# A float32 attention and two gated layers on one core: the v_in product as seven block products per pair of row blocks, the v_out product in four parts of K

## The chip, the cores and the metric

The kernel runs on one core of a Trainium2 chip. The metric is the device time of one execution in microseconds (us); several runs are timed and their median is compared. Engines: TensorE (PE; its weight loads are the row PEld), VectorE (DVE), ScalarE (ACT), GpSimd (POOL) and SyncE (SP), whose queue issues all the DMAs of this kernel.

## What is computed

Causal attention over 2 batches, 12 heads, 448 positions and head size 64 gives x (896 tokens by 768). Two layers follow; in the kernel w_out of the first is already folded into its w3, and the names v_in and v_out stand for `moe2_w_in` and `moe2_w_out`.

```python
def _moe_ref(x, w1, w2, w3, w_out):
    a = x @ w1
    b = x @ w2
    h = a * b @ w3
    return (h @ w_out).astype(np.float32)

def _moe2_ref(x, w_in, w_out):          # w_in 768 x 2048, w_out 2048 x 768
    h = x @ w_in
    relu6 = np.clip(h + 3.0, 0.0, 6.0)
    g = h * relu6 / 6.0
    return (g @ w_out).astype(np.float32)
```

The products keep float32 accuracy on TensorE by splitting every operand into a high and a low part in the float32r type, so that each 128x128 block product is three matmuls (high times high, high times low, low times high). The weights arrive as 64-bit floats; ScalarE and VectorE put the bits together.

## The kernel before, in words

All activations are held transposed: features on the 128 partitions, tokens along the free axis, in two batches b of S = 448 columns. One matmul therefore moves 448 columns through a 128x128 weight block.

The program records every operation in a `Plan` with an engine, an estimated cost, its reads and writes and a rank. `Plan.issue` then plays a list schedule with these costs and writes the instructions out in the order that it finds; each engine runs its own queue strictly in that order. Work of the last layers has rank `DENSE + n`, with n the index of a weight unit in the list `units`. `ahead(n)` fetches unit n + 3 and converts unit n + 2 after unit n.

The stages, in order:

- Attention, with the product of w3 and w_out (`weights_product`, tile pw) beside it and after it.
- The product with w1 and w2, tiles paX, paY and paZ (`first`, `second`, `multiply`). Here both are already computed as a 2x2 block product with seven block products: a pair consists of one block column of w1 and one of w2, the inner dimension of 768 falls into two halves of HK = 3 blocks, and the two batches are the other side. `combine` forms the block sums of the weights (S1 to S4, A11, A12, A22) and `moving` those of the activations (tiles T1 to T4). P1 to P7 in `side` name which is multiplied by which; one of them is 3 blocks times 3 matmuls.
- The product px with the folded weights (tile wp, line 770), three groups of two row blocks and two batches in four PSUM banks; `keep` (lines 645 to 651) splits each result into the high and low parts of x2t, by a ScalarE copy (line 647) and a VectorE subtraction (line 649).
- The product with v_in, tile pg (line 635): 16 row blocks m, 2 batches, KD = 6 blocks, 3 matmuls, each result going through `hswish` (ScalarE, VectorE, ScalarE, VectorE, lines 656 to 662) into gt[m], of which all 16 are kept.
- The product with v_out, tile po (line 811): 6 row blocks, two halves of KF = 8 blocks, 2 batches, 3 matmuls; the 16 blocks of K accumulate in one PSUM bank, and `store` copies it out (lines 669 and 671) and sends it by DMA (line 673).

Converting one unit of v_in takes two operations on VectorE and one on ScalarE for the bits (`bits`: lines 279, 286, 289) and one on each for the split (`split`: lines 259 and 261). The tiles "raw" (RAWS = 3) hold what a DMA brought, the tiles "hl" (HLS = 4) what is ready for TensorE; in `combine` the second of a pair has a tile "raw2" with two buffers. PSUM has 8 banks, 2 in the pool `pd` (tag "d") and 6 in the pool of tag "dl". The pair of tiles "a1" and that of "a2" are scratch for results on their way.

Of the kernel before, what the change touches and what calls it, by code (L numbers as in the profile page):

```python
# [34 lines left out]
DENSE = 100.0  # L35
# [6 lines left out]
EARLY, LATE = 0, 1.0  # L42
# [112 lines left out]
def attention_moe_moe2(ctx: ExitStack, tc, q, k, v, w1, w2, w3, w_out, v_in, v_out, out):  # L155
# [19 lines left out]
    HK = KD // 2  # L175
    SCALE = 1.0 / float(D) ** 0.5
# [55 lines left out]
    def fetch(plan, n, rank):  # L232
# [4 lines left out]
        if name == "w2":  # L237
            raw = plan.tile(lambda: later["t"].tile([P, KD * P, 2], U32, tag="raw2", name=f"{name}r{m}", bufs=2),
                            "raw2", 2, (done,))
            raw2s.append(raw)  # L240
        else:
            raw = plan.tile(lambda: ws.tile([P, KF * P, 2], U32, tag="raw", name=f"{name}r{m}", bufs=RAWS), "raw", RAWS)
# [50 lines left out]
    def convert(plan, n, rank):  # L293
# [3 lines left out]
        if name == "w1":  # L297
            return
        raw, size = raws.pop(n)
        if name == "w2":  # L300
            combine(plan, m, raws.pop(n - 1)[0], raw, rank)
# [15 lines left out]
    def combine(plan, f, r1, r2, rank):  # L317


        size, h = KD * P, KD * P // 2  # L320
        bits(plan, r1, size, rank, True)
        low = lambda r, i, k=1: f32(r[:, i * h:(i + k) * h, 0])
        high = lambda r, i, k=1: f32(r[:, i * h:(i + k) * h, 1])
        first, second, third, fourth = (parts(f"{c}", f) for c in ("wa", "wb", "wc", "wd"))
        split(plan, first, 0, size, lambda: low(r1, 0, 2), [r1.at("l")], rank)
        bits(plan, r2, size, rank, True)

        def add(eng, dst, reads, write, a, b, op):
# [300 lines left out]
    def product(ps, n, kt, x, keys):  # L629
        hl = hls[n]  # L630
        mm = list(passes(kt))
        for kk in range(kt):
            def go(kk=kk):
                for _, a, c, st, sp in mm[3 * kk:3 * kk + 3]:
                    nc.tensor.matmul(ps[:, :S], weight(n, a, kk), x(kk, c), start=st, stop=sp)  # L635

            plan.op("pe", 0.6, go, reads=[hl, *keys(kk)], writes=[ps], rank=DENSE + n)

# [6 lines left out]
    def keep(ps, t, b, n):  # L645

        plan.op("act", act(S), lambda: nc.scalar.copy(part(t, HI, b), ps[:, :S]),
                reads=[ps], writes=[t.at((b, HI))], rank=DENSE + n)
        plan.op("dve", dve(S), lambda: nc.vector.tensor_tensor(
            part(t, LO, b), ps[:, :S], f32(part(t, HI, b)), ALU.subtract),  # L650
            reads=[ps, t.at((b, HI))], writes=[t.at((b, LO))], rank=DENSE + n)

    def hswish(ps, t, m, b, n):
        r = scratch("a1", f"r_{m}_{b}")
        g6 = scratch("a2", f"g6_{m}_{b}")
        plan.op("act", act(S), lambda: nc.scalar.activation(r[:, :], ps[:, :S], AF.Relu, bias=three, scale=1.0),  # L656
# [224 lines left out]
```

## Time and profile before

| | us |
|---|---|
| median of 3 runs | 572.93 |
| the three runs | 573.76, 572.93, 569.14 |
| the profiled execution's own time | 571.27 |
| its span, from the first to the last instruction | 569.3 |

The profile comes from one execution. The time of that execution is 1.97 us longer than its span. In the profile's views a matmul's start is measured and its end is modelled, so two matmuls that follow each other overlap in their rows; the distance of their starts is what one costs. TensorE's granted clock is given as a share of 2.4 GHz.

### The profile page before, as it was taken

The page shows a single profiled execution, that of the slowest core. Times are in us where ns is not written, and L with a number is a line of the kernel's source. Part 1 is how long each engine was busy: PE and PEld are TensorE (multiplying, and loading weights), DVE is VectorE, ACT ScalarE, POOL GpSimd, SP SyncE. Part 2 cuts the span into 40 slices and gives each one's busy share as a digit, 9 for nine tenths or more (in the row PEclk, how much of TensorE's full clock was granted, in tenths as well). Part 3 has the DMA queues.
Part 4 walks back from the last instruction along what each step waited for, and adds up shares of the span by engine and source line. Part 5 has one row for each costly group of instructions (what it writes and reads, how often), then busy time and mean ns, then how long its engine had stood idle before and what let it go on. Part 6 is the DMA issues. An engine that isn't in the chain of part 4 may idle for free.

```text
span 569.3 us, 7756 instructions
## 1 busy us (share of the span) xinstructions
PE 555.1 (98%) x2900; PEld 494.1 (87%) x2900; DVE 326.1 (57%) x583; ACT 283.2 (50%) x556; POOL 111.8 (20%) x142
## 2 busy tenths in 40 slices
PE   6899999999999999999999999999999999999997
PEld 4576757878999998999999999999999999999996
DVE  3677776855952978887633547666667643331000
ACT  4587877776815557764331335555556522220100
POOL 4556546642140323331000000000000000000000
PEclk8799999999999999999999999999999999999999
DMA  8666685724514233321603324333243433430000
GB/s 318 225 196 220 224 276 200 237 71 129 170 50 139 93 125 115 112 94 37 202 1 112 111 76 145 108 114 109 101 153 124 143 149 119 152 107 16 17 32 33
DMA packets 22853, 73.38 MB, mean 129 GB/s; under 512 B 2080, under 2 KB 11296, under 8 KB 20256
## 3 DMA queue, kind: packets, MB, share of 16 engines
q1 hardware_dynamic: 22816, 72.88, 37.8%
q8 instruction: 23, 0.38, 0.3%
q14 instruction: 14, 0.11, 0.1%
HBM read 66.98 MB, written 5.90 MB: 128 GB/s over the span
## 4 chain that ended last, share of the span: by engine, by line
PE 70%; DVE 3%; DMA 2%; ACT 1%; issue 0%; ACTq 0%; DVEq 0%; SPq 0%
PE po L811 20%; PE pg L635 20%; PE px L770 10%; PE pw L553 7%; PE paX L696 7%; PE paZ L696 3%; PE paY L696 2%; DMA w1r<-in_moe_w 1%; DVE wd L261 1%; DMA w2r<-in_moe_w 1%; DVE w1r L289 1%; DVE ab L724 0%; DVE w1r L330 0%; PE o L490 0%; PE ptp L465 0%; ACT w1r L279 0%
## 5 line engine op out<-in xcount | busy, mean ns | idle before, releaser
L635 PE MATMUL pg<-x2t,vi 128*128 128x448 f32 x576 | 115.4, 362 | 0.0
L811 PE MATMUL po<-g,vo 128*128 128x448 f32 x576 | 115.4, 362 | 0.0
L635 PEld LDWEIGHTS pg<-x2t,vi 128*128 128x128 f32 x576 | 108.0, 188 | 7.2
L811 PEld LDWEIGHTS po<-g,vo 128*128 128x128 f32 x576 | 108.0, 188 | 7.2
L553 PE MATMUL pw<-wr,w 128*128 128x384 f32 x384 | 75.8, 347 | 0.0
L443 POOL TENSOR_SCALAR prb<-prb,sums 128x448 f32<-128x448 f32 (+6 forms) x84 | 59.7, 727 | 54.9 <-DVE sums L437 52.2
L553 PEld LDWEIGHTS pw<-wr,w 128*128 128x128 f32 x384 | 66.0, 188 | 1.7
L770 PE MATMUL px<-ab,wp 128*128 128x448 f32 x288 | 57.9, 362 | 0.0
L416 PE MATMUL s<-ks,qs 128*128 128x448 f32 (+6 forms) x168 | 53.2, 428 | 4.1 <-DMA ks<-in_k 3.3
L770 PEld LDWEIGHTS px<-ab,wp 128*128 128x128 f32 x288 | 54.0, 188 | 3.6
L423 ACT ACTIVATE prb<-z,sums 128x448 f32<-128x448 f32 (+6 forms) x84 | 42.1, 506 | 5.7 <-DVE sums L419 5.5
L416 PEld LDWEIGHTS s<-ks,qs 128*128 128x128 f32 x168 | 29.4, 203 | 14.9 <-DVE sums L419 5.1
L419 DVE CUSTOM_DVE_ANT_0 z<-s,maskb 128x448 f32<-128x448 f32 (+6 forms) x84 | 33.2, 418 | 15.1 <-PE s L416 8.6
L656 ACT ACTIVATE r<-pg,consts 128x448 f32<-128x448 f32 x32 | 20.3, 635 | 33.2 <-PE pg L635 33.2
L279 ACT ACTIVATE vor<-vor 128x1024 f32<-128x1024 f32 x12 | 14.0, 1164 | 36.9 <-DMA vor<-in_moe_w_out 36.9
L473 ACT COPY pt<-ptp 128x512 f32<-128x512 f32 (+1 forms) x48 | 24.7, 561 | 14.9 <-PE ptp L465 14.7
L658 DVE SCALAR_TENSOR_TENSOR g<-r,pg 128x448 f32<-128x448 f32 x32 | 19.8, 619 | 19.7 <-ACT r L656 19.6
L465 PEld LDWEIGHTS ptp<-ident,prb 128*128 128x128 f32 x192 | 22.0, 141 | 10.0 <-POOL prb L443 5.0
L465 PE MATMUL ptp<-ident,prb 128*128 128x128 f32 x192 | 25.9, 276 | 4.3 <-POOL prb L443 4.2
L490 PE MATMUL o<-pt,vr 128*64 128x448 f32 (+3 forms) x192 | 26.9, 396 | 0.0
L669 ACT COPY out<-po 128x448 f32<-128x448 f32 x6 | 3.2, 534 | 47.1 <-PE po L811 29.3
L671 DVE COPY out<-po 128x448 f32<-128x448 f32 x6 | 3.8, 627 | 39.8 <-PE po L811 39.8
(103 smaller groups left out, 786.7 us busy)
## 6 DMA issues: line engine op xcount, KB each, us to landing
vir<-in_moe_w_in SPq DMA_DIRECT2D x16, 768.0 KB, 4.3
vor<-in_moe_w_out SPq DMA_DIRECT2D x12, 1024.0 KB, 4.9
w3r<-in_moe_w SPq DMA_DIRECT2D x8, 1024.0 KB, 6.7
wrr<-in_moe_w_out SPq DMA_DIRECT2D x8, 768.0 KB, 5.9
w1r<-in_moe_w SPq DMA_DIRECT2D x8, 768.0 KB, 5.8
w2r<-in_moe_w SPq DMA_DIRECT2D x8, 768.0 KB, 4.3
qs<-in_q SPq DMA_DIRECT2D x12, 448.0 KB, 3.4
vr<-in_v SPq DMA_DIRECT2D x12, 256.0 KB, 3.4
```

The lines of the kernel that those rows point to most:

```text
L416: plan.op("pe", pe4(n), lambda: nc.tensor.matmul(ps[:, :n], qs[u][:, t].rearrange("p h i -> p (h i)"), ks[u][:, :n], start=True, stop=True ...
L419: plan.op("dve", dve(n) + 0.09, lambda: nc.vector.tensor_tensor_reduce(out=z[:, :n], in0=ps[:, :n], in1=maskb[:, S - n:], scale=-SCALE, sc ...
L423: plan.op("act", act(n, True) + 0.2, lambda: nc.scalar.activation(pb[:, OFF[t]:OFF[t] + n], z[:, :n], AF.Exp, bias=sm[:, 0, t:t + 1], scal ...
L443: nc.gpsimd.tensor_scalar(s, s, sm[:, 1, t:t + 1], 1.0, ALU.mult, ALU.mult)
L465: nc.tensor.transpose(ps[:w, i * P:(i + 1) * P], pb[:, OFF[t] + kb * P:OFF[t] + kb * P + w], ident)
L473: plan.op("act", act(cut), lambda: nc.scalar.copy(dst()[:, :cut], ps[:, :cut]), reads=[ps], writes=[d.at((g, 0))], rank=rank)
L490: nc.tensor.matmul(ps[T * j:T * j + T, kb * P:S], vr[u][:w, kb, j, :], d[:w, base[kb]:base[kb] + TQ - 2 * kb, j, :], start=kb == 0, stop=k ...
L553: nc.tensor.matmul(ps[:, :W], weight(n, a, kk), hls[1 + kk][:, c, h * W:(h + 1) * W], start=kk == 0 and a == c, stop=kk == KF - 1 and a == LO)
L635: nc.tensor.matmul(ps[:, :S], weight(n, a, kk), x(kk, c), start=st, stop=sp)
L696: nc.tensor.matmul(ps[:, :S], hl[:, a, off + kk * P:off + (kk + 1) * P], t[:, c], start=first and kk == 0 and a == c, stop=kk == HK - 1 an ...
L770: nc.tensor.matmul(ps[m, b][:, :S], weight(n, a, kk), ab[kk][:, c, cols(b)], start=kk == 0 and a == c, stop=kk == KF - 1 and a == LO)
L811: nc.tensor.matmul(ps[:, :S], weight(n, a, kk), gt[k][:, c, cols(b)], start=k == 0 and a == c, stop=k == KF2 - 1 and a == LO)
```

## The change

The product with v_in takes the form that the product with w1 and w2 already has. Row blocks 2f and 2f + 1 of v_in make a pair (units "vi" and "vj"), eight pairs in all, and `gated(f)` computes both row blocks for both batches by P1 to P7 in three PSUM banks X, Y and Z, with sums on the way taken by ScalarE copies (`keep_sum`) and VectorE additions (`add_sum`). The 2x2 blocks of x2 come from px: its groups are now rows p and p + 3 together, and `differences` forms T1 to T4 from the four PSUM banks of a group and a scratch tile x2s, beside the three blocks of x2t that are needed as they are.

`combine` serves both products. For v_in ("vj") its four additions all run on VectorE, its two wide high-part copies on GpSimd (before, the additions of w1 and w2 are half on GpSimd and the copies on ScalarE), and three of the seven weight blocks (S2, A22, S4) go into tiles of one buffer each (`own`).

The product with v_out is cut into four parts c of KC = 4 blocks of K. Part c needs only the pairs 2c and 2c + 1, so gt shares the buffers of ab, 8 blocks instead of 16. The list `work` sets the order: pairs 0 and 1; then for each part the next pair, a third of part c - 1, the next pair, and the two other thirds; at the end the three thirds of the last part. A third is two row blocks m and one unit of v_out in a new layout (512 rows by 256 columns). Since a bank no longer holds the whole sum, `evict` copies the result of part 0 to a tile o (ScalarE) and writes it to DRAM (`sums_of`); for parts 1 to 3 o is fetched from DRAM first, VectorE adds the bank to it, and it goes back to DRAM or, in the last part, to the output.

`hswish` works in place on one scratch tile and reads its input from SBUF for three of the four results of a pair. The SBUF set aside for descriptors of dynamic DMAs is halved (1024 instead of 2048). The functions `product` and `store`, the old loops over m and `turn3` are gone. The diff, cut to its core:

```diff
+    KC = 4
+    NC = KF2 // KC
...
-    units += [(None, KF, m, "wp") for m in range(KD)]
-    units += [(v_in, KD, m, "vi") for m in range(KF2)]
-    units += [(v_out, KF, n, "vo") for n in range(2 * KD)]
-    raws, hls, comb, raw2s = {}, {}, {}, []
+    units += [(None, KF, m, "wp") for p in range(HK) for m in (p, p + HK)]
+    work = [("pg", 0), ("pg", 1)]
+    for c in range(1, NC):
+        work += [("pg", 2 * c), ("po", c - 1, 0), ("pg", 2 * c + 1), ("po", c - 1, 1), ("po", c - 1, 2)]
+    work += [("po", NC - 1, i) for i in range(HK)]
+    for w in work:
+        first_of[w] = len(units)
+        if w[0] == "pg":
+            units += [(v_in, KD, 2 * w[1], "vi"), (v_in, KD, 2 * w[1] + 1, "vj")]
+        else:
+            units.append((v_out, KF, w[2] * NC + w[1], "vo"))
...
-        if name == "w2":
+        if name in ("w2", "vj"):
...
+        beside = f[0] == "vj"
+        adds, eng = (("dve",) * 4, "pool") if beside else (ADDS, "dve")
...
+        def own(i):
+            return plan.tile(lambda: xp.tile([P, 2, S], F32R, tag=f"x{i}_1", name=f"v{i}_{f[1]}"), f"x{i}_1", 1)
+        first, second = (parts(f"{f[0]}{c}", f[1]) for c in "ab")
+        if beside:
+            s2, a22, s4 = ((own(i), 0) for i in range(3))
+        else:
+            s2, a22 = ((parts(f"{f[0]}{c}", f[1]), 0) for c in "cd")
+            s4 = a22[0], h
+        split(plan, first, 0, size, lambda: low(r1, 0, 2), [r1.at("l")], rank, eng)
...
+        split(plan, *s2, h, lambda: high(r1, 0), [H1], rank)
+        split(plan, second, 0, size, lambda: high(r2, 0, 2), [H2], rank, eng)
+        split(plan, *a22, h, lambda: low(r2, 1), [L2], rank)
+        split(plan, *s4, h, lambda: high(r1, 1), [H1], rank)
...
+    def evict(ps, m, b, n, c, o):
+        rank = DENSE + n
+        if c:
+            plan.op("dve", dve(S), lambda: nc.vector.tensor_tensor(o[:, :], ps[:, :S], o[:, :], ALU.add),
+                    reads=[ps], writes=[o], rank=rank)
+        else:
+            plan.op("act", act(S), lambda: nc.scalar.copy(o[:, :], ps[:, :S]), reads=[ps], writes=[o], rank=rank)
+        if c == NC - 1:
+            plan.op("sp", 0.6, lambda: nc.sync.dma_start(out[m * P:(m + 1) * P, cols(b)], o[:, :]),
+                    reads=[o], rank=rank)
+        else:
+            plan.op("sp", 0.6, lambda: nc.sync.dma_start(sums_of[m, b], o[:, :]),
+                    reads=[o], writes=[summed.at((m, b))], rank=rank)
...
+    def multiply(f, name, ps, first, rank, kind="w2"):
         a, *x = side[name]
-        hl, off = comb[f][a]
+        hl, off = comb[kind, f if kind == "w2" else 2 * f + 1][a]
+        xs = xt if kind == "w2" else x2
...
+    def differences(p, ps, rank):
+        s = plan.tile(lambda: xp.tile([P, 2, S], F32, tag=f"x{p}_1", name=f"x2s{p}"), f"x{p}_1", 1)
+        low, high = s.at(0), s.at(1)
+        plan.op("act", act(S), lambda: nc.scalar.copy(s[:, 0], ps[p, 1][:, :S]), reads=[ps[p, 1]], writes=[low], rank=rank)
+        for m, b in ((p, 0), (p + HK, 0), (p + HK, 1)):
+            x2[m, b] = plan.tile(
+                lambda m=m, b=b: xp.tile([P, 2, S], F32R, tag=f"x{m}_{b}", name=f"x2t{m}_{b}"), f"x{m}_{b}", 1)
+            keep(ps[m, b], x2[m, b], rank)
+        def less(i, bank, j):
+            plan.op("dve", dve(S), lambda: nc.vector.tensor_tensor(s[:, i], bank[:, :S], s[:, j], ALU.subtract),
+                    reads=[bank, s.at(j)], writes=[s.at(i)], rank=rank)
+        def whole(name, i):
+            t = plan.tile(lambda: later["t"].tile([P, 2, S], F32R, tag=f"{name}_{p}", name=f"{name}g_{p}"),
+                          f"{name}_{p}", 1, (done,))
+            plan.op("act", act(S, True), lambda: nc.scalar.copy(t[:, HI], s[:, i]),
+                    reads=[s.at(i)], writes=[t.at(0)], rank=rank)
+            plan.op("dve", dve(S), lambda: nc.vector.tensor_tensor(t[:, LO], s[:, i], f32(t[:, HI]), ALU.subtract),
+                    reads=[s.at(i), t.at(0)], writes=[t.at(1)], rank=rank)
+            tt[name, p] = t
+        less(1, ps[p + HK, 1], 0)
+        plan.op("dve", dve(S), lambda: nc.vector.tensor_tensor(s[:, 0], s[:, 0], ps[p, 0][:, :S], ALU.subtract),
+                reads=[ps[p, 0]], writes=[low], rank=rank)
+        whole("T1", 0)
+        less(0, ps[p + HK, 1], 0)
+        whole("T3", 1)
+        whole("T2", 0)
+        less(1, ps[p + HK, 0], 0)
+        whole("T4", 1)
...
+    sums_of = dp.tile([KD, B, P, S], F32, name="sums_of")
+    summed = Handle(plan, None, None, 0)
+    summed.ap = sums_of
...
+    def gated(f):
+        rank = DENSE + first_of["pg", f]
+        for m in (2 * f, 2 * f + 1):
+            tag = f"ab{m % KF}"
+            gt[m] = plan.tile(lambda m=m, tag=tag: later["ab"].tile([P, 2, NT], F32R, tag=tag, name=f"g{m}"),
+                              tag, 1, (done2,))
+        X, Y, Z = (dense_bank(f"pg{c}{f}") for c in "XYZ")
+        p1, c22, u2 = scratch("a1", f"q1_{f}"), scratch("a1", f"q22_{f}"), scratch("a2", f"q2_{f}")
+        def keep_sum(bank, x):
+            plan.op("act", act(S), lambda: nc.scalar.copy(x[:, :], bank[:, :S]), reads=[bank], writes=[x], rank=rank)
+        def add_sum(bank, x):
+            plan.op("dve", dve(S), lambda: nc.vector.tensor_tensor(x[:, :], x[:, :], bank[:, :S], ALU.add),
+                    reads=[bank], writes=[x], rank=rank)
+        multiply(f, "P1", X, True, rank, "vj")
+        keep_sum(X, p1)
+        multiply(f, "P2", Y, True, rank, "vj")
+        add_sum(Y, p1)
+        hswish(lambda: p1[:, :], p1, gt[2 * f], 0, rank + LATE)
+        multiply(f, "P6", X, False, rank, "vj")
+        keep_sum(X, u2)
+        multiply(f, "P5", Z, True, rank, "vj")
+        keep_sum(Z, c22)
+        multiply(f, "P7", X, False, rank, "vj")
+        add_sum(X, c22)
+        hswish(lambda: c22[:, :], c22, gt[2 * f + 1], 1, rank + LATE)
+        multiply(f, "P3", Z, False, rank, "vj")
+        add_sum(Z, u2)
+        hswish(lambda: u2[:, :], u2, gt[2 * f], 1, rank + LATE)
+        multiply(f, "P4", X, False, rank, "vj")
+        hswish(lambda: X[:, :S], X, gt[2 * f + 1], 0, rank)
+    def collected(c, i):
+        n = first_of["po", c, i]
+        for j in range(2):
+            m = 2 * i + j
             for b in range(B):
+                name = f"po{c}_{m}_{b}"
+                ps = dense_bank(name) if j else plan.tile(
+                    lambda name=name: pd.tile([P, 512], F32, tag="d", name=name), "psd", DENSE_BANKS)
+                o = scratch("a2", f"o{c}_{m}_{b}") if b else spare(f"o{c}_{m}_{b}")
+                if c:
+                    plan.op("sp", 0.6, lambda o=o, m=m, b=b: nc.sync.dma_start(o[:, :], sums_of[m, b]),
+                            reads=[summed.at((m, b))], writes=[o], rank=DENSE + n - 2)
+                for kk in range(KC):
+                    def go(ps=ps, n=n, at_=(kk * 2 + j) * P, k=c * KC + kk, kk=kk, b=b):
+                        for a, d in ((HI, HI), (HI, LO), (LO, HI)):
                             nc.tensor.matmul(
+                                ps[:, :S], hls[n][:, a, at_:at_ + P], gt[k][:, d, cols(b)],
+                                start=kk == 0 and a == d, stop=kk == KC - 1 and a == LO)
+                    plan.op("pe", 0.6, go, reads=[hls[n], *halves(gt[c * KC + kk], b)], writes=[ps], rank=DENSE + n)
+                evict(ps, m, b, n, c, o)
+    for w in work:
+        if w[0] == "pg":
+            gated(w[1])
+            for i in range(2):
+                ahead(first_of[w] + i)
+        else:
+            collected(*w[1:])
+            ahead(first_of[w])
     plan.issue()
+    right.close()
+    left.close()
...
+    if name == "moe2_w_out":
+        return _units(a, 512, 256)
```

The order of the instructions, as the planner writes it out. TensorE, where px ends and the product with v_in begins (px_0 and px_1 are banks of px by batch, wp and vi weights, x2t the activations; each row is three matmuls), before:

```order
L770 MATMUL px_1_3027<-ab_2780,wp_2889 128x448 x3
L770 MATMUL px_1_3033<-ab_2780,wp_2907 128x448 x3
L635 MATMUL pg_0_3141<-x2t_0_2871,vi_3017 128x448 x3
L635 MATMUL pg_0_3141<-x2t_0_2876,vi_3017 128x448 x3
L635 MATMUL pg_0_3141<-x2t_0_2999,vi_3017 128x448 x3
L635 MATMUL pg_0_3141<-x2t_0_3004,vi_3017 128x448 x3
L635 MATMUL pg_0_3141<-x2t_0_3127,vi_3017 128x448 x3
L635 MATMUL pg_0_3141<-x2t_0_3132,vi_3017 128x448 x3
```

And now, from the third row of the stage on (vja holds the blocks A11 and A12 of a pair, vjb S1 and S3, v_1 the block S2 of the first pair, T1g and T2g the block sums of x2):

```order
L708 MATMUL pgX_3195<-x2t_0_3178,vja_3049 128x448 x3
L708 MATMUL pgY_3212<-x2t_0_2891,vja_3049 128x448 x3
L708 MATMUL pgY_3212<-x2t_0_3041,vja_3049 128x448 x3
L708 MATMUL pgY_3212<-x2t_0_3184,vja_3049 128x448 x3
L708 MATMUL pgX_3195<-T2g_2961,v_1_2990 128x448 x3
L708 MATMUL pgX_3195<-T2g_3102,v_1_2990 128x448 x3
L708 MATMUL pgZ_3240<-T1g_2944,vjb_3058 128x448 x3
L708 MATMUL pgZ_3240<-T1g_3088,vjb_3058 128x448 x3
L708 MATMUL pgZ_3240<-T1g_3228,vjb_3058 128x448 x3
L708 MATMUL pgX_3257<-x2t_0_2885,vja_3192 128x448 x3
L708 MATMUL pgX_3257<-x2t_0_3036,vja_3192 128x448 x3
L708 MATMUL pgX_3195<-T2g_3249,v_1_2990 128x448 x3
```

The six blocks of x2t of one batch stood one after the other; now P1 and P2 take three each, and T2g and T1g, which are made from the last results of px, come 18 matmuls behind its end. Two rows of the next pair (vja_3192) are drawn ahead of the last block of T2g, which is the 14th row of the stage.

VectorE at the same place, before (x2t are the low parts of the last px group, vi the low part of a unit of v_in, vir its bits):

```order
L649 TENSOR_TENSOR x2t_0_3127<-px_0_3013,x2t_0_3127 128x448
L649 TENSOR_TENSOR x2t_0_3132<-px_0_3020,x2t_0_3132 128x448
L649 TENSOR_TENSOR x2t_1_3138<-px_1_3027,x2t_1_3138 128x448
L261 TENSOR_TENSOR vi_3145<-vir_2939,vi_3145 128x768
L649 TENSOR_TENSOR x2t_1_3159<-px_1_3033,x2t_1_3159 128x448
L261 TENSOR_TENSOR vi_3165<-vir_3038,vi_3165 128x768
L658 SCALAR_TENSOR_TENSOR g_0_0_3189<-r_0_3184,pg_0_3141 128x448
L662 SCALAR_TENSOR_TENSOR g_3194<-g_0_0_3189,g_3194 128x448
L286 TENSOR_SCALAR vir_3171<-vir_3171 128x768
```

And now, from the second instruction on the last px group on (x2s is the scratch tile of `differences`, q_0 the sum of the first pair's P1 and P2):

```order
L658 TENSOR_TENSOR x2t_0_3184<-px_0_3060,x2t_0_3184 128x448
L350 TENSOR_TENSOR vir_2963<-vjr_3133,vir_2963 128x384
L658 TENSOR_TENSOR x2t_1_3199<-px_1_3070,x2t_1_3199 128x448
L788 TENSOR_TENSOR x2s_3190<-px_1_3070,x2s_3190 128x448
L801 TENSOR_TENSOR x2s_3190<-x2s_3190,px_0_3052 128x448
L270 TENSOR_TENSOR vja_3192<-vir_2928,vja_3192 128x768
L796 TENSOR_TENSOR T3g_3222<-x2s_3190,T3g_3222 128x448
L796 TENSOR_TENSOR T1g_3228<-x2s_3190,T1g_3228 128x448
L788 TENSOR_TENSOR x2s_3190<-px_1_3070,x2s_3190 128x448
L788 TENSOR_TENSOR x2s_3190<-px_0_3060,x2s_3190 128x448
L846 TENSOR_TENSOR q_0_3216<-q_0_3216,pgY_3212 128x448
L796 TENSOR_TENSOR T2g_3249<-x2s_3190,T2g_3249 128x448
```

Four subtractions for x2t with two weight operations among them have become thirteen operations up to the last block of T2g.

## Rows read from the trace of the kernel before

**Rows 1.** The chain that ended last: start us, length us, engine, tile, line.

```profile
...
277.86 57.00 PE px L770 x285
334.86 115.20 PE pg L635 x576
450.05 115.21 PE po L811 x576
...
565.34 0.53 ACT out L669
```

**Rows 2.** Busy time in four stretches: length, each engine's busy us, clock, DMA share, GB/s.

```profile
223.00:277.00 54.00, 53.62 (x269) 50.27 (x269) 44.07 (x61) 32.58 (x52) 12.45 (x10) 1.00 0.33 116
...
335.00:450.00 115.00, 115.00 (x577) 107.81 (x576) 78.35 (x113) 65.04 (x96) 0.00 (x0) 1.00 0.39 130
450.00:565.00 115.00, 115.00 (x577) 107.71 (x575) 29.15 (x31) 21.45 (x23) 0.00 (x0) 1.00 0.22 78
```

**Rows 3.** Groups by line: busy us, mean ns of one, idle before and releaser.

```profile
L289 DVE SCALAR_TENSOR_TENSOR vir<-vir 128x768 uint32<-128x768 uint32 x16 | 15.3, 956 | 3.9 <-ACT vir L279 3.9
L261 DVE TENSOR_TENSOR vi<-vir,vi 128x768 fp32r<-128x768 f32 x16 | 15.3, 954 | 1.1 <-ACT vi L259 1.1
...
L261 DVE TENSOR_TENSOR wc<-w1r,wc 128x384 fp32r<-128x384 f32 x8 | 4.4, 549 | 0.9 <-ACT wc L259 0.9
...
L662 DVE SCALAR_TENSOR_TENSOR g<-g,g 128x448 fp32r<-128x448 f32 x32 | 19.9, 622 | 9.7 <-ACT g L660 9.7
...
L649 DVE TENSOR_TENSOR x2t<-px,x2t 128x448 fp32r<-128x448 f32 x12 | 7.3, 623 | 22.5 <-ACT x2t L647 22.5
...
L289 DVE SCALAR_TENSOR_TENSOR vor<-vor 128x1024 uint32<-128x1024 uint32 x12 | 14.7, 1224 | 3.0 <-ACT vor L279 2.9
...
L286 DVE TENSOR_SCALAR vor<-vor 128x1024 uint32<-128x1024 uint32 x12 | 8.3, 694 | 20.6 <-DMA vor<-in_moe_w_out 20.6
...
L255 POOL TENSOR_SCALAR wr<-wrr 128x768 fp32r<-128x768 f32 x8 | 6.6, 830 | 0.0
```

**Rows 4.** Instructions of VectorE and GpSimd in order of time: start us, length us.

```profile
231.87 0.61 DVE L714 TENSOR_TENSOR u<-u,paZ 128x448 f32<-128x448 f32 x1
...
232.40 0.55 DVE L261 TENSOR_TENSOR wd<-w2r,wd 128x384 fp32r<-128x384 f32 x1
232.62 1.34 POOL L716 TENSOR_TENSOR u<-u,c 128x448 f32<-128x448 f32 x1 [2.03 <-DVE u L714]
232.87 1.51 DVE L261 TENSOR_TENSOR wd<-w1r,wd 128x384 fp32r<-128x384 f32 x1
...
234.76 0.95 DVE L261 TENSOR_TENSOR wa<-w1r,wa 128x768 fp32r<-128x768 f32 x1
...
235.63 0.61 DVE L724 TENSOR_TENSOR ab<-u,ab 128x448 fp32r<-128x448 f32 x1
```

**Rows 5.** Instructions at the end of px, in order of time.

```profile
334.69 10.56 PE L635 MATMUL pg<-x2t,vi 128*128 128x448 f32 x52
...
335.52 0.54 ACT L647 CAST x2t<-px 128x448 fp32r<-128x448 f32 x1
...
336.53 0.62 DVE L649 TENSOR_TENSOR x2t<-px,x2t 128x448 fp32r<-128x448 f32 x1
```

**Rows 6.** DMA issues: count, KB each, median us from issue to landing.

```profile
vir<-in_moe_w_in SPq DMA_DIRECT2D x16, 768.0 KB, 4.3
vor<-in_moe_w_out SPq DMA_DIRECT2D x12, 1024.0 KB, 4.9
...
ks<-in_k SPq DMA_DIRECT2D x12, 224.0 KB, 3.6
out<-out SPq DMA_DIRECT2D x12, 224.0 KB, 1.9
```

**Rows 7.** The tile ks (224 KB a load, in the attention stages): its loads.

```profile
DMA to landing us min/median/max: 3.3/3.6/8.6
```

More of the change, by code (lines that the diff above doesn't have):

```diff
@@ L627, in cols @@
         return slice(b * S, (b + 1) * S)
[L629 to L637, printed above, removed]
     def halves(t, b):
@@ L643, in part, with keep @@
         return t[:, i, cols(b)] if t.tag[0] in "ag" else t[:, i, :]
[L645 to L656, printed above, removed]
-                reads=[ps], writes=[r], rank=DENSE + n)
+    def keep(ps, t, n):
+        plan.op("act", act(S), lambda: nc.scalar.copy(t[:, HI], ps[:, :S]), reads=[ps], writes=[t.at(HI)], rank=n)
+        plan.op("dve", dve(S), lambda: nc.vector.tensor_tensor(t[:, LO], ps[:, :S], f32(t[:, HI]), ALU.subtract),
+                reads=[ps, t.at(HI)], writes=[t.at(LO)], rank=n)
@@ L679, in users @@
+    ab, open_ = {}, {}
     def users(handles):
@@ L701, in multiply, with spare @@
             plan.op("pe", 0.6, go, reads=[hl, t], writes=[ps], rank=rank)
+    def spare(name):
+        return plan.tile(lambda: later["t"].tile([P, S], F32, tag="c22", name=name, bufs=2), "c22", 2, (done,))
     def second(f):
@@ L705, in second @@
         rank = rank_of(min(f + 1, KF - 1))
-        early = f < EARLY
-        pool_of, ready = ("t", done) if early else ("ab", done2)
-        ab[f] = plan.tile(lambda: later[pool_of].tile([P, 2, NT], F32R, tag=f"ab{f}", name=f"ab{f}"), f"ab{f}", 1, (ready,))
+        ab[f] = plan.tile(lambda: later["ab"].tile([P, 2, NT], F32R, tag=f"ab{f}", name=f"ab{f}"), f"ab{f}", 1, (done2,))
         multiply(f, "P4", X, False, rank)
@@ L731, in first @@
         p1, u2 = scratch("a1", f"p1_{f}"), scratch("a2", f"u2_{f}")
-        c22s.append(plan.tile(lambda: later["t"].tile([P, S], F32, tag="c22", name=f"c22_{f}", bufs=2), "c22", 2, (done,)))
-        c22 = c22s[-1]
+        c22 = spare(f"c22_{f}")
         multiply(f, "P1", X, True, rank)
@@ L772, in go @@
                             start=kk == 0 and a == c, stop=kk == KF - 1 and a == LO)
-                plan.op("pe", 0.6, go, reads=[hls[n + m - m0], *halves(ab[kk], b)],
+                plan.op("pe", 0.6, go, reads=[hls[n + (m != p)], *halves(ab[kk], b)],
                         writes=[ps[m, b]], rank=DENSE + n)
-        for m, b in group:
-            x2[m, b] = plan.tile(
-                lambda m=m, b=b: xp.tile([P, 2, S], F32R, tag=f"x{m}_{b}", name=f"x2t{m}_{b}"), f"x{m}_{b}", 1)
-            keep(ps[m, b], x2[m, b], b, n)
+        differences(p, ps, DENSE + n)
         ahead(n)
```

90 lines of the change are left out of this document (24 added, 66 removed).

## Prediction

> **What bounds the kernel now.** I read the chain that ended last first, because only what stands in it can shorten the run. From 277.86 us on it holds nothing but matmuls: 285 of px, 576 of pg, 576 of po, and then one copy and the last store [rows 1]. Next I read the busy time by stretch, to see whether anything else is near. TensorE is busy 115.00 of 115 us in pg and the same in po, at a granted clock of 1.00 (the level of 2.4 GHz); VectorE 78.35 and 29.15 us, ScalarE 65.04 and 21.45, GpSimd not at all [rows 2]. So the last 288 us are worth what their matmuls cost, and work on the other engines is free until it stands in front of a matmul. The reader is to keep two numbers: 576 matmuls take 115.20 us, 0.200 each [rows 1], and VectorE has 85 us of idle time in po that pg does not have.
>
> **What goes.** The v_in product had 16 x 2 x 6 x 3 = 576 matmuls. A pair by seven products has 7 x 3 x 3 = 63, eight pairs 504. The 72 that go are worth 72 x 0.200 = 14.4 us. That the new form runs at the same pace is shown by the stretch in which w1 and w2 are already done so: 269 matmuls in 53.62 us busy, 0.199 each, while VectorE is busy for 44.07 of 54 us [rows 2]. The v_out product keeps its number: 4 parts x 12 banks x 4 blocks x 3 = 576. The two together should take 1080 x 0.200 = 216.0 us where they took 230.4.
>
> **What is added on VectorE.** Per pair, from rows of the same size [rows 3]: two combinations of bits at 0.956, two wide low parts at 0.954, four additions and three small low parts of 384 columns at 0.549, which is 7.7 us; three sums from PSUM at 0.623 and eight steps of the gate at 0.622, 6.8 us. Together 14.5 us for a pair that TensorE does in 63 x 0.200 = 12.6. These are single durations; when VectorE has its next instruction ready, starts are closer: 0.53 for 448 columns (231.87 to 232.40), 0.47 for 384 (232.40 to 232.87), 0.87 for 768 (234.76 to 235.63) [rows 4]. By these a pair comes to 4 x 0.87 + 7 x 0.47 + 11 x 0.53 = 12.6. So VectorE is no faster than TensorE inside a pair. What saves it is v_out: a third of a part is 48 matmuls, 9.6 us, and costs VectorE 0.694 + 2 x 1.224 for its weights and 4 x 0.623 for the additions, 5.6 us [rows 3]. Two pairs and three thirds are 54.0 us of TensorE and 29.0 + 16.9 = 45.9 of VectorE, 85%.
>
> GpSimd gets 16 copies at 0.830 [rows 3], two per pair, and VectorE pays for some. While GpSimd ran an addition of 1.34 us, a VectorE instruction of 384 columns took 1.51 us where the same one took 0.55 just before [rows 4]; 0.96 us were lost to it. No row has the one-input copy against VectorE at leisure, so its price is between 0 and its whole length: 0 to 1.66 us per pair. With the upper end a pair costs VectorE 16.2 us and a part 49.3 of 54.0, 91%. I take about half, by the nearest row, in which most of the GpSimd time was lost. On the path that is still nothing as long as the thirds carry it.
>
> The Trainium skill says of this, on the page SBUF — State Buffer, in the section on who interferes with whom, that a VectorE instruction with two SBUF inputs and a GpSimd instruction that reads SBUF exclude each other, the later one blocking fully. The rows before agree for additions; for a copy none of them decides. By the rule all 16 x 0.830 = 13.3 us would be lost on VectorE, which speaks against this change and leads to the first rival below.
>
> **Where px ends.** Before, the next matmul follows at once (334.69), although the last low part of x2t starts only at 336.53 [rows 5]. Now the last block of T2g is wanted 13 rows of three matmuls after px, 7.8 us, by TensorE's order. On VectorE's order, between the last px bank and that block, stand a ScalarE copy of 0.54 [rows 5], then nine steps of 448 columns at 0.622 and one of 768 at 0.954: 0.54 + 5.6 + 0.95 = 7.1 us. That just fits; closely spaced it is 6.2. Two GpSimd copies fall in this time; if both block, 8.8 us. The stall is 0 to 1.0 us and I take 0.5. Ahead of these steps VectorE also combines bits of a DMA that needs 4.3 us [rows 6]; by the same kind of sum it is done about 1 us before px ends, and a late one would add its lateness.
>
> **The first two pairs** have no third behind them. From T2g to the low part of the first v_out unit VectorE has 33 instructions, 22.2 us by single durations [rows 3]; with four GpSimd copies 25.5. That is 7.1 + 25.5 = 32.6 us after px, and TensorE wants it 57 rows of three after px, 34.2 us. Behind it the next pair's weights are wanted 13 us later. I take 0.2 us for waits here; the bounds are 0 and the price of the first rival.
>
> **The sums through DRAM.** 36 stores and 36 loads of 224 KB are new on SyncE's queue, 16.5 MB. The rows of that size are 3.6 us for a load and 1.9 for a store [rows 6]. Each o tile is one of two per batch, so it comes round every four banks, 9.6 us; load, addition and store take 3.6 + 0.6 + 1.9 = 6.1. A late one is covered by PSUM: a bank of tag "d" is wanted again only 7.2 us after its last matmul. Cost 0; if a load lands as slowly as 1 MB of weights, 4.9 us [rows 6], it is still 7.4. The end is as before, with a VectorE addition (0.623) where a ScalarE copy stood (0.53) [rows 1, 3]: 0.1 us.
>
> **Sum.** 571.27 (the profiled execution) - 14.4 + 0.5 + 0.2 + 0.1 = 557.7 us. The median of the runs shown lies 1.66 us above that execution, so I predict 559.3.
>
> **Rivals.**
>
> First, VectorE is late in the opening. The copies on GpSimd block it in full, and pairs 0 and 1, which have no third of v_out to hide in, run at VectorE's 16.2 us instead of 12.6: 2 x 3.6 = 7.2 us. With the other terms that is 564.9, by the median 566.5. For it: VectorE's 85 to 91% and in-order waits for ScalarE (9.7 us before line 662 alone [rows 3]). Against it: VectorE starts the stage with the first pair's weights largely done under px.
>
> Second, and slower: every pair is paced by VectorE. S2, A22 and S4 have one buffer each, so the next pair's small parts wait for P6, P4 and P3 of this one; if the planner's queue then leaves nothing for the thirds, each pair costs 16.2 - 12.6 = 3.6 us more, eight of them 28.8, and the time is 571.27 - 14.4 + 28.8 = 585.7, by the median 587.4. It beats the gain from 1.8 us per pair on. For it: the one buffer. Against it: behind six of the eight pairs stands at least 9.6 us of v_out, and the w1 and w2 stage ran 0.199 per matmul with VectorE at 82% [rows 2].
>
> Third, no change: the ring of o tiles is the bound. If every load lands as late as the slowest of that size, 8.6 us [rows 7], a round is 8.6 + 0.6 + 1.9 = 11.1 us instead of 9.6; 36 banks are nine rounds, 13.5 us, and the time is 571.2, by the median 572.8. For it: loads stand behind stores and behind 1 MB of weights on one queue. Against it: that slowest load came under the DMA load of the attention, while here the DMAs are busy 22 to 39% [rows 2].
>
> **How the numbers follow.** Forecast 0.80, first rival 0.10, second 0.04, third 0.06. The forecast's own range is 555 to 565: the fastest run shown less 14.4, and the upper ends of the stalls. The range of 8 in 10 reaches to the first rival and a little past it, 555 to 568. A measurement of this kernel tells about 1% from no change, here 567.2. Faster by more than 1%: 0.80 + 0.08 of the first rival = 0.88; within 1%: 0.07; slower: 0.05.
>
> **What would show it.** In the changed profile the chain should hold only matmuls from px to the end, pg 504 and po 576 of them at 0.200, with a break of under 2 us where px ends. Right in each step: VectorE busy for at most 8 x 14.5 + 12 x 3.1 + 36 x 0.62 = 176 us, less what it does under px, with GpSimd copies beside stretched low parts; o loads of 3 to 5 us. The forecast is wrong if the chain passes through VectorE low parts of vja, vjb or v for more than 5 us in all (first or second rival), if VectorE waits for o and TensorE for a bank (third), or if the clock falls below 1.00 in the stage.

## The result, and the profile after

| | before | changed |
|---|---|---|
| median, us | 571.61 of 4 runs | 555.47 of 4 runs |
| runs | 569.14 to 573.76 | 555.24 to 559.55 |
| profiled execution | 571.27 | 559.55 |

The changed kernel is faster: ratio 0.9753, 95% interval 0.9712 to 0.9793, which is 14.1 us of 571.6 (11.8 to 16.5). (The medians lie 16.1 us apart.) The profiled execution is the slowest of the four: its mean granted clock is 0.991 over the whole run, that of the other three 0.996 to 0.997. Where its time went is read first, since that decides which numbers can be compared. These are the first 30 us of it by engine (length; busy us of PE, PEld, DVE, ACT, POOL with counts; granted clock; DMA share; GB/s):

```profile
0.00:30.00 30.00, 23.44 (x94) 16.20 (x95) 14.63 (x48) 15.36 (x42) 15.17 (x34) 0.83 0.71 259
```

And the same stretch in another execution of the same kernel, the first run of the experiments:

```profile
0.00:30.00 30.00, 25.28 (x121) 18.14 (x121) 18.37 (x60) 18.68 (x54) 16.77 (x36) 0.94 0.76 274
```

The one got 94 matmuls done at a mean granted clock of 0.83, the other 121 at 0.94 (1.00 is 2.4 GHz; both means hold some time at the lower level). What was lost there stayed lost: the final run of px matmuls starts at 279.34 and at 274.85 us. Over the ten profiles of this study it starts at 277.86 to 279.40 where the mean clock of the first 30 us is 0.83 (three profiles), at 273.75 to 276.76 where it is 0.94 (six), and at 273.42 where it is 1.00 (one). These stages lie ahead of the two that the change is about. So a difference of one or two us between totals says little here. What is compared below is the stretch from the end of px to the last matmul, read from the chain of waits: before, 334.86 to 565.26, 230.4 us [rows 1].

The chain of the changed kernel from px on: start us, length us, engine, tile, line. Shown are the opening, the sixth pair in full and the end:

```profile
279.34 57.00 PE px L817 x285
336.34 1.80 PE pgX L708 x9
...
438.79 1.80 PE pgX L708 x9
440.59 1.80 PE pgY L708 x9
442.39 1.86 PE pgX L708 x9
444.25 1.81 PE pgZ L708 x9
446.06 1.80 PE pgX L708 x9
447.86 1.86 PE pgZ L708 x9
449.72 1.86 PE pgX L708 x9
...
506.13 48.02 PE po L882 x240
```

It holds matmuls from px to the last copy, as before, and no break where px ends. The stretch is 336.34 to 554.15: 217.8 us, 12.6 less than before and 1.8 more than 1080 x 0.200 = 216.0. Each row of the pair is one block product of nine matmuls, in the order P1, P2, P6, P5, P7, P3, P4. Four of them take the 1.80 us that 9 x 0.200 gives, P6, P3 and P4 take 1.86. That 0.06 is no slip of the clock, which is 1.00 throughout: it returns in P6, P3 and P4 of every pair, 24 times, and makes 1.44 of the 1.8 us.

The groups by line, by tile: busy us, mean ns of one, idle before:

```profile
L708 PE MATMUL pgX<-T2g,v 128*128 128x448 f32 x72 | 16.3, 368 | 0.0
L708 PE MATMUL pgZ<-x2t,v 128*128 128x448 f32 x72 | 16.2, 369 | 0.0
...
L708 PE MATMUL pgX<-x2t,vja 128*128 128x448 f32 x72 | 15.9, 362 | 0.0
```

The three slow products (the third, pgX<-T4g,v, has a mean of 367) are those that read their weights from a tile v, the tiles that `own` makes; those from vja and vjb have a mean of 362 to 364 ns. (Such a mean overlaps with the next matmul's; what counts is the difference of 5 to 7 ns.)

Busy time by stretch, in the columns of [rows 2]; the first line is the opening:

```profile
335.00:360.00 25.00, 25.00 (x125) 23.20 (x124) 23.26 (x38) 17.72 (x33) 3.88 (x4) 1.00 0.31 106
335.00:450.00 115.00, 115.00 (x571) 106.69 (x570) 100.77 (x152) 81.64 (x132) 11.95 (x12) 1.00 0.52 179
450.00:553.60 103.60, 103.60 (x517) 96.53 (x516) 57.76 (x87) 29.30 (x43) 1.82 (x2) 1.00 0.57 183
```

VectorE has 158.5 us of work behind px where it had 78.35 + 29.15 = 107.5 [rows 2]. In the opening it is busy for 93% of the time, and TensorE for all of it.

VectorE, GpSimd and TensorE where px ends (start us, length us):

```profile
336.68 1.19 POOL L264 TENSOR_SCALAR vjb<-vjr 128x768 fp32r<-128x768 f32 x1
337.05 0.61 DVE L658 TENSOR_TENSOR x2t<-px,x2t 128x448 fp32r<-128x448 f32 x1
...
340.03 0.96 POOL L264 TENSOR_SCALAR vja<-vir 128x768 fp32r<-128x768 f32 x1 [2.16 <-PE pgY L708]
340.17 1.29 DVE L796 TENSOR_TENSOR T1g<-x2s,T1g 128x448 fp32r<-128x448 f32 x1
...
343.22 0.62 DVE L796 TENSOR_TENSOR T2g<-x2s,T2g 128x448 fp32r<-128x448 f32 x1
...
344.00 0.78 PE L708 MATMUL pgX<-T2g,v 128*128 128x448 f32 x3
```

The last block of T2g is done at 343.84, 7.5 us after px; its matmuls start at 344.00, right behind six matmuls of the next pair. It fits by 0.2 us. T1g, with both inputs in SBUF, took 1.29 us beside a GpSimd copy, the same subtraction T2g 0.62 without one; x2t, which reads one input from PSUM, kept its 0.61 beside the copy of 336.68.

The DMA issues: count, KB each, median us from issue to landing:

```profile
sums_of<-o SPq DMA_DIRECT2D x36, 224.0 KB, 2.9
o<-sums_of SPq DMA_DIRECT2D x36, 224.0 KB, 2.7
```

A load of o lands after 2.7 us, below the 3.6 of ks in [rows 6]; a store of a partial sum takes 2.9 instead of the 1.9 of a store to the output.

### The profile page after: what moved, and what is told of

The parts are those of the page before. It is cut to its first block, busy times and chain, and to the rows that moved or that the text cites. A ratio compares the mean times of both kernels' runs of the same rounds, so it can differ in the third digit from the quotient of the medians.

```text
span 557.8 us, 7964 instructions
## 1 busy us (share of the span) xinstructions
PE 543.3 (97%) x2828; PEld 481.2 (86%) x2828; DVE 387.9 (70%) x698; ACT 315.0 (56%) x622; POOL 128.5 (23%) x158
## 4 chain that ended last, share of the span: by engine, by line
PE 69%; DVE 3%; DMA 2%; ACT 1%; issue 0%; ACTq 0%; DVEq 0%; SPq 0%
PE po L882 21%; PE pgX L708 11%; PE px L817 10%; PE pw L573 7%; PE paX L708 7%; PE pgZ L708 5%; PE paZ L708 3%; PE pgY L708 3%; PE paY L708 2%; DMA w1r<-in_moe_w 1%; DVE w2d L270 1%; DMA w2r<-in_moe_w 1%; DVE w1r L298 1%; DVE ab L737 0%; DVE w1r L350 0%; PE o L510 0%
## 5 line engine op out<-in xcount | busy, mean ns | idle before, releaser
L676 DVE TENSOR_TENSOR o<-po,o 128x448 f32<-128x448 f32 x36 | 22.5, 624 | 41.0 <-PE po L882 40.8
L439 DVE CUSTOM_DVE_ANT_0 z<-s,maskb 128x448 f32<-128x448 f32 (+6 forms) x84 | 33.3, 418 | 16.3 <-PE s L436 11.8
L264 POOL TENSOR_SCALAR vja<-vir 128x768 fp32r<-128x768 f32 x8 | 7.3, 916 | 152.3 <-DVE x2t L658 51.9
L485 PEld LDWEIGHTS ptp<-ident,prb 128*128 128x128 f32 x192 | 23.2, 146 | 10.1 <-POOL prb L463 5.2
L350 POOL TENSOR_TENSOR w2r<-w2r 128x384 f32<-128x384 f32 x8 | 12.4, 1554 | 70.3 <-DVE w2r L298 58.5
L510 PEld LDWEIGHTS o<-pt,vr 128*64 128x64 f32 (+1 forms) x192 | 10.9, 134 | 17.5 <-issue 11.6
L268 ACT CAST vo<-vor 128x1024 fp32r<-128x1024 f32 x12 | 13.7, 1139 | 17.5 <-PE po L882 14.9
L669 DVE SCALAR_TENSOR_TENSOR g<-rab,g 128x448 fp32r<-128x448 f32 x32 | 20.5, 649 | 1.6 <-ACT g L667 1.6
```

Of the source, the lines that this page charges most:

```text
L439: plan.op("dve", dve(n) + 0.09, lambda: nc.vector.tensor_tensor_reduce(out=z[:, :n], in0=ps[:, :n], in1=maskb[:, S - n:], scale=-SCALE, sc ...
L485: nc.tensor.transpose(ps[:w, i * P:(i + 1) * P], pb[:, OFF[t] + kb * P:OFF[t] + kb * P + w], ident)
L510: nc.tensor.matmul(ps[T * j:T * j + T, kb * P:S], vr[u][:w, kb, j, :], d[:w, base[kb]:base[kb] + TQ - 2 * kb, j, :], start=kb == 0, stop=k ...
L676: plan.op("dve", dve(S), lambda: nc.vector.tensor_tensor(o[:, :], ps[:, :S], o[:, :], ALU.add), reads=[ps], writes=[o], rank=rank)
```

## The experiments

The experiments ran in two batches, on two chips. All ratios are against the kernel before in the same batch (median 569.80 of 11 runs in the first, 569.24 of 19 in the second). The second batch (all pairs first, the parts alone, no sums fetched back, one ring) has no run of the changed kernel; its kernels are compared with it by their ratios and by the stretch. "The stretch" is always end of px to last matmul.

**The changed kernel again, and the own tiles moved.** The theory: the three slow products come from where S2, A22 and S4 lie. In the built program's allocation every tile "hl" starts at 160 bytes modulo 256 within a partition; the activations x2t, the tiles T1 to T4 and the own tiles all start at 224. Only where weights come from an own tile do the weights and the moving operand stand at the same place modulo 256. The edit puts the weights 48 columns (192 bytes) further into their tiles, at 160:

```diff
-            s2, a22, s4 = ((own(i), 0) for i in range(3))
+            s2, a22, s4 = ((own(i), 48) for i in range(3))
```

> The changed kernel as it is, once more, so that the next ones stand beside it on one chip. Both theories: 555 to 560 us, 0.975 of the kernel before; from the end of px to the last matmul 217.8 us, of which groups of nine matmuls with the weights S2, S4 and A22 take 1.86 us and all others 1.80.

> The three small weight blocks S2, A22 and S4 stand 48 columns (192 bytes) further right in their tiles, so that they lie at the same address modulo 256 as all other weights (160) and no longer at that of the moving operands (224). Theory A (weights and moving operand at the same place modulo 256 cost a matmul 6.7 ns): their groups of nine go from 1.86 to 1.80 us, 24 of them, 1.4 to 1.6 us less in all. Theory B (these groups are late for their single buffer or for a semaphore): nothing changes, 1.86 stays.

The changed kernel: median 556.39 of 6, ratio 0.9772 (0.9737 to 0.9807). Moved: 556.38 of 6, ratio 0.9777 (0.9741 to 0.9813). The chain of the moved one, P1, P6 and P3 of the sixth pair and the end:

```profile
437.80 1.80 PE pgX L708 x9
...
441.40 1.80 PE pgX L708 x9
...
446.80 1.80 PE pgZ L708 x9
...
504.99 48.02 PE po L882 x240
```

P6 (441.40) and P3 (446.80) take 1.80. With px ending at 336.40 the stretch is 216.6 us, against 217.8 in the first profile and 219.3 in the one of this batch; a mean of 363 or less stands in all seven groups of products. The place of the tiles is the cause of the 206.7 ns. The stretch is 1.2 and 2.7 us shorter than in the two profiles: 1.44 by the 24 groups, and the waits are 0.6 us here against 0.4 and 1.9 there. The medians don't show it, since the runs of each spread over more than 4 us. The 0.6 us left above 216.0 are one wait of TensorE, where P7 follows ScalarE's copy of bank X after P6 (line 843).

The repeated kernel had 1.9 us of its own above 216.0 + 1.44. Its chain leaves TensorE in two places. The first costs 1.5 us:

```profile
408.05 7.57 DMA vor<-in_moe_w_out
...
415.70 1.15 ACT vor L288
416.85 0.41 ACT q L843
...
417.31 2.09 PE pgX L708 x9
```

And the waits of PE behind px (us in total, times, longest):

```profile
PE pgX L708 <- ACT q L843: 1.3, 1, 1.3
```

A load of v_out weights came 7.57 us after its issue, where the median is 5.3; ScalarE stood before it, idle for 3.28 us, and the copy of P1 out of bank X (line 843), on which P6 waits, stood behind in its queue although P1 was complete. That is an in-order queue at work, at 417 us, far behind the opening. The second place, at 471 us, costs 0.3 us: there the copy stood behind a step of the gate that waited for VectorE's sum.

**All pairs first.** Is it the thirds of v_out between the pairs that keep VectorE from being the bound? The list is put in the plain order; since gt has only 8 blocks, parts 0 and 1 read the gate blocks 8 to 15 again, so v_out computes something else, with the same matmuls.

```diff
-    work = [("pg", 0), ("pg", 1)]
-    for c in range(1, NC):
-        work += [("pg", 2 * c), ("po", c - 1, 0), ("pg", 2 * c + 1), ("po", c - 1, 1), ("po", c - 1, 2)]
-    work += [("po", NC - 1, i) for i in range(HK)]
+    work = [("pg", f) for f in range(2 * NC)]
+    work += [("po", c, i) for c in range(NC) for i in range(HK)]
```

> Only the order is changed: all eight pairs in a row, then the twelve thirds of v_out. For that the first two parts read the gate's blocks 8 to 15 a second time in place of 0 to 7 (this part of the result is left out). Theory A (VectorE has 12.6 to 14.5 us of work per pair against TensorE's 12.6, and it is the thirds that carry it): TensorE stalls inside the pairs, 2 to 12 us slower than the changed kernel, and the chain of the pairs passes through VectorE. Second rival of the prediction (16.2 us per pair): 25 to 29 us slower. Third theory (the order does not matter, VectorE keeps up by itself): within 1 us.

Median 560.86 of 4, ratio 0.9824 (0.9774 to 0.9874). The stretch of the eight pairs, in the columns of [rows 2]:

```profile
330.75:436.96 106.21, 103.91 (x506) 93.89 (x505) 101.75 (x165) 77.75 (x135) 14.98 (x14) 1.00 0.30 105
```

Part of its chain:

```profile
393.95 1.94 PE pgX L706 x9
395.98 2.53 POOL vjb L262
398.54 0.96 DVE vjb L268
```

VectorE is busy for 101.75 of 106.21 us, 96%: 12.7 us per pair, what was left over from px included. It first stands in the chain at 380.07, at the end of the fourth pair; the last four pairs take 55.1 us by TensorE's starts (381.73 to 436.80), 13.8 each. A GpSimd copy stands in the chain once, with 2.53 us where the same kind took 0.83 in [rows 3]. Eight pairs cost 504 x 0.200 + 1.44 = 102.2 without a wait, so the order of the list is worth 4.0 us in this execution, about 1.0 for each pair of the second half; the ratio is 0.5% above that of the changed kernel, 3.0 us. It matters, but a pair paced by VectorE costs 13.8 us, not the 16.2 of the rivals.

The order also spreads the transfers. With all thirds in a row, loads and stores of o take a median of 3.9 us each, against 2.7 and 2.9 in the changed kernel, and VectorE waits 30.9 us for o, in 21 waits. TensorE still waits for none of it: the 576 matmuls take 115.2 us.

**The parts alone.** v_out in four parts with the sums through DRAM, but v_in as before (16 row blocks, 576 matmuls).

```diff
-            units += [(v_in, KD, 2 * w[1], "vi"), (v_in, KD, 2 * w[1] + 1, "vj")]
+            units += [(v_in, KD, 2 * w[1] + i, "vx") for i in range(2)]
...
+            for b in range(B):
+                ps = dense_bank(f"pg{m}_{b}")
+                for kk in range(KD):
...
+                hswish(lambda ps=ps: ps[:, :S], ps, gt[m], b, DENSE + n)
```

> The v_out product in four parts with its sums through DRAM, between the row blocks of v_in as before the change (16 blocks, 2 batches, 6 x 3 matmuls, no seven products). Theory A (the parts and the DRAM sums cost nothing, and the gain is the 72 matmuls): the time of the kernel before, ratio 1.00 within 0.005. Rival (the parts themselves gain or lose): a ratio away from 1.00 by more than that.

Median 569.17 of 10, ratio 0.9989 (0.9963 to 1.0015). The end of its chain, all matmuls:

```profile
501.21 14.40 PE pg L818 x72
515.61 48.01 PE po L839 x240
```

The stretch is 333.21 to 563.62, 230.4 us as before. The parts, the 72 DMAs and the additions cost nothing and gain nothing. The whole gain of the stretch is the 72 matmuls, less the 1.44 us of the slow groups and what the pairs wait.

**No sums fetched back.** The loads of o and the additions are left out, so the output holds only the last part; ScalarE copies every bank out, 36 copies in place of VectorE's 36 additions.

```diff
-        if c:
+        if False:
...
-                if c:
+                if False:
```

> The partial sums are not fetched back and not added: every bank is copied out by ScalarE and stored (the sum over the four parts is left out of the result). Takes 36 loads and 36 VectorE additions away. Theory A (they are hidden): within 1 us of the changed kernel. Third rival of the prediction (the ring is felt): faster by more than 2 us.

Median 557.66 of 4, ratio 0.9780 (0.9726 to 0.9834); the stretch is 333.76 to 552.40, 218.6 us. Nothing is gained against the 217.8 and 219.3 of the changed kernel: the reload is hidden.

**One ring for o.** How much room does the ring have? Both batches take their o from one pair of tiles, so a tile comes round after two banks (4.8 us) instead of four (9.6).

```diff
-                o = scratch("a2", f"o{c}_{m}_{b}") if b else spare(f"o{c}_{m}_{b}")
+                o = spare(f"o{c}_{m}_{b}")
```

> The tiles o of both batches share one ring of two buffers in place of one ring of two for each batch. By the prediction's model of the ring (load 2.7, addition 0.6, store 2.9 us by the changed kernel's trace, 6.2 in all) a buffer now comes round every two banks, 4.8 us, so that each round is 1.4 us late where thirds follow each other: the last 20 banks alone lose 10 rounds, 10 to 16 us slower than the changed kernel. If transfers are hidden whatever the ring is: 0 to 1 us.

Median 574.82 of 10, ratio 1.0084 (1.0057 to 1.0112). Part of its chain in the last banks (SPq is SyncE's queue):

```profile
526.34 2.77 DMA sums_of<-o
...
529.13 0.32 SPq L877
...
529.50 2.83 DMA out<-o
...
532.35 0.32 SPq L877
```

Store, issue of the next load, and again, 3.2 to 3.3 us per bank. (The load and the addition of the other tile pass at the same time.) The last 20 banks take 65.2 us, 500.77 to 565.95, instead of 48.0, and the stretch 235.5 instead of 217.8. A round of one tile is thus 2 x 3.25 = 6.5 us: load 2.7, addition 0.6, store 2.9, and 0.32 for the issue that my 10 to 16 us had left out. In the changed kernel the round has 9.6 us, so 3.1 us are to spare.

**The GpSimd copies on ScalarE.** The wide high parts of v_in are made by ScalarE, as for w1 and w2.

```diff
-        adds, eng = (("dve",) * 4, "pool") if beside else (ADDS, "dve")
+        adds, eng = (("dve",) * 4, "dve") if beside else (ADDS, "dve")
```

> The sixteen wide high-part copies of v_in run on ScalarE, GpSimd is out of the stage. Theory A (TensorE bounds everything after px, the lock between GpSimd and VectorE is covered): the time stays within 1 us of the changed kernel, while VectorE rows that were stretched beside a copy (T1g 1.29 us, vir 0.85) come back to 0.62 and 0.55. Rival (the lock decides in the opening): 2 us or more faster.

Median 557.05 of 4, ratio 0.9777 (0.9735 to 0.9819); stretch 218.9 us. VectorE's two groups of the gate behind px, in this run:

```profile
L669 DVE SCALAR_TENSOR_TENSOR g<-rab,g 128x448 fp32r<-128x448 f32 x32 | 19.6, 620 | 1.4 <-ACT g L667 1.3
L665 DVE SCALAR_TENSOR_TENSOR rab<-rab,q 128x448 f32<-128x448 f32 x24 | 14.8, 618 | 0.0
```

The same two, and the copies themselves, in the changed kernel:

```profile
L669 DVE SCALAR_TENSOR_TENSOR g<-rab,g 128x448 fp32r<-128x448 f32 x32 | 20.5, 649 | 1.6 <-ACT g L667 1.6
L665 DVE SCALAR_TENSOR_TENSOR rab<-rab,q 128x448 f32<-128x448 f32 x24 | 16.2, 675 | 0.0
...
L264 POOL TENSOR_SCALAR vjb<-vjr 128x768 fp32r<-128x768 f32 x7 | 7.4, 1054 | 25.5 <-PE pgX L708 6.9 <-ACT rab L663 6.6 <-issue 4.7
L264 POOL TENSOR_SCALAR vja<-vir 128x768 fp32r<-128x768 f32 x7 | 6.4, 919 | 117.8 <-PE po L882 39.4 <-DVE vir L298 38.0 <-PE pgY L708 23.0
```

VectorE loses 0.9 and 1.4 us in these groups and 0.67 in T1g. Other groups lose too, the wide low parts of vja above all: over the same 272 instructions, from 36 us before the end of px to the last matmul, it is busy for 180.2 us in the first profile of the changed kernel (180.8 in the second) and for 176.4 here, 3.8 to 4.3 us in all. The copies themselves stretch from 830 [rows 3] to 919 and 1054 ns. None of it is on the path, and moving the copies to ScalarE gains nothing.

**Without the gap.** A tile of 64 bytes named "gap" stands ahead of the activations. Without it the activations start at 160 modulo 256, as the "hl" tiles do, while T1 to T4 stay at 224. If a matmul at an equal place takes 206.7 ns, then px, po, P1 and P2 become slow, P3 stays slow, and P6 and P4 become fast.

```diff
-    gap.tile([P, 16], F32, name="gap")
```

> The 64-byte tile gap is left out, so that xt, x2t, ab and gt lie at 160 modulo 256 as the weights in hl do; T1 to T4 stay at 224. Theory A: the 1296 matmuls with one of these as moving operand and weights from hl (px 288, P1 to P3 of both seven-product stages 432, po 576) cost 6.7 ns more each, 8.7 us, P6 and P4 of the pairs lose their 6.7 ns (1.0 us less), and the weights product pw may slow by up to 2.6 us: 7 to 11 us slower than the changed kernel. Theory B: no change.

Median 560.18 of 4, ratio 0.9833 (0.9790 to 0.9875). Part of its chain:

```profile
276.73 58.90 PE px L816 x285
...
439.21 1.86 PE pgX L707 x9
...
442.93 1.80 PE pgX L707 x9
...
448.33 1.86 PE pgZ L707 x9
...
507.31 49.61 PE po L881 x240
```

These are slow: px 58.90 / 285 = 206.7 ns, P1 (439.21), P2 and P3 (448.33) 1.86 us, po 49.61 / 240 = 206.7, and P6 (442.93) is back at 1.80. From the start of px to the last matmul it takes 280.2 us where the changed kernel took 274.8 in its first profile (276.3 in the second, with its 1.9 us of waits). My expectation was too high: P3 is slow with and without the gap, and P6 and P4 give back what P1 and P2 lose, so only px (1.9) and po (576 x 0.0067 = 3.9) are left there, 5.8 us, against 5.4 measured. The stage of w1 and w2 lies ahead of that and adds 216 x 0.0067 = 1.4 (its P1 to P3 take 1.86 too). The weights product pw, whose operands now stand at the same place as well, adds nothing: 219 of its matmuls, of 384 columns, take 38.16 us in the chain here and 38.17 in the changed kernel. The median is only 3.8 us above that of the changed kernel, under my 7 to 11; what is missing is less than the starts of the profiles vary by.

## Why the prediction was right, and where not

- **The 72 matmuls.** Right: the chain has 504 of pg and 576 of po, and with the v_in part of the change alone undone the time is that of before.
- **"The new form runs at the same pace".** This is the step that was off: the term of 14.4 us was mis-sized. Four of the seven products run at 0.200; P6, P3 and P4, whose weights lie in own tiles, run at 0.2067. That is 24 x 0.06 = 1.44 us, so the term is 13.0. The row I took it from, the stretch of w1 and w2, reads its weights from "hl" tiles only. That S2, A22 and S4 go into other tiles stood in the diff; I weighed their one buffer, and not their place.
- **The stall where px ends, 0.5.** The last block of T2g came 7.5 us after px against 7.1 forecast, and the matmuls that want it came 0.2 us later; the stall was 0, the lower bound. That the 7.1 fits so well is partly luck: the steps start closer than their single durations, which the 0.67 us lost in T1g and short waits made up for.
- **The first two pairs, 0.2.** Here too nothing. Waits came elsewhere and differ from execution to execution: above 216.0 + 1.44 the stretch has 0.4 us in the first profile and 1.9, 1.4 and 1.2 in those of the repeated kernel, of the copies on ScalarE and of the kernel without the reload. Forecast were 0.7 for both stalls together. In each of the last three the chain leaves TensorE for one of ScalarE's copies out of a bank (line 843), for which the sum had no term: the copy stood behind a late load of weights in the repeated kernel (v_out, 7.57 us) and in the one without the reload (v_in 6.85, v_out 6.58), and behind VectorE's sum and ScalarE's other work with the copies on ScalarE.
- **VectorE.** 158.5 us behind px against at most 176 forecast; the pair costs 12.7 (all pairs first), the value of the close spacing, so the thirds were worth 4.0 us and not the 28.8 of the second rival. That rival's mechanism is there in the order with all pairs first, at a price of about 1.0 us for half of the pairs; the point from which it would beat the gain was 1.8 for each.
- **GpSimd's copies.** Forecast about half of the time lost on VectorE; found were 3.8 to 4.3 us, of 16 copies with 13.3 us by their length before. The first rival falls with it: TensorE has no wait in the first two pairs. The 13.3 in full, which I took from the rule of the Trainium skill (SBUF — State Buffer, on who interferes with whom), went further than the rule does: the page limits it to VectorE instructions with two SBUF inputs, and either side can be the one that waits. The trace agrees with that: T1g took 1.29 us beside a copy, x2t with one input in PSUM kept 0.61, and the copies themselves were stretched.
- **The sums through DRAM, 0.** Right, shown by the kernel without the reload and by the one with the parts alone. The round is 6.5 us where I had 6.1; a load came sooner, a store later, and the issue was missing. The third rival falls: the ring becomes the bound at half its size.
- **The base.** The forecast was 559.3 and the median 555.47, though the sum of changes (-13.6) was larger than what the two profiles show from px to the last matmul (-12.6). The rest is the level: I added the sum to 572.93, the median of three runs, and the kernel before has a median of 571.61 with one run more, and 569.80 (11 runs) and 569.24 (19) in the two batches of experiments. From 569.80 the same sum gives 556.2, and 556.39 was measured beside it. That level goes with the clock of the first 30 us, by the starts of px above, and not with the change.

What stays open: by the ratios the change is worth 14.1 us (11.8 to 16.5) in the first comparison and 2.28% of 569.80, 13.0 us, in the second, and the stretch accounts for 11.1 to 12.6. The remainder is within what the start of the run varies, but no run shows that it is only that: in the first batch the runs whose mean granted clock is 0.996 or 0.997 (seven before, three changed) differ by 13.2 us on average.

## What to carry to other kernels

Where TensorE is the bound, matmuls that are dropped come back almost in full as long as the other engines' work has stretches to spread into: here the order of the work list, pairs with v_out between them, was worth 4.0 us, while the transfers that it needed cost nothing because their ring of tiles had 3 us to spare. With all thirds in a row the same transfers took longer, 3.9 us each, though still hidden. Take a pace from a row with the same operands in the same tiles; a new home for the weights is a change of its own. And with a start that varies by 6 us, compare a stretch of the chain rather than the totals when one or two us are in question.

## What the runs showed that I had not expected

In these kernels a matmul of 448 columns costs 206.7 ns instead of 200.0 when its weights and its moving operand start at the same place modulo 256 bytes in a partition. The matmuls of pw, of 384 columns, showed no such cost (174.3 ns either way), and no run varies the length alone. Two edits show it from both sides: 192 bytes on the weights take it away in P6, P3 and P4, and 64 bytes fewer ahead of the activations bring it to px, po, P1 and P2 and take it from P6 and P4. Whether it is 256 or 128 that counts can't be told, since 160 and 224 differ under both. It isn't 64, by which all of them are equal. It isn't 512 either: by that, two of the three matmuls of each block of P6 stand at an equal place but only one of the three in P3, and both products take 1.86 us. Why it costs 6.7 ns no run shows. The version with the tiles moved has the shortest stretch of all (216.6 us), but its median doesn't differ from the changed kernel's by what can be measured.
